# One core, attention and a token mixer in one kernel: the same 2,292 operations in another written-out order

## The chip, the cores and the metric

The kernel runs on one core of one Trainium2 chip. The metric is the device time of one execution in microseconds (us). Lower is better. A profile of one execution is at hand for the kernel before, with the time of each instruction on each engine: TensorE (PE, with its weight loads as PEld), VectorE (DVE), ScalarE (ACT), GpSimd (POOL), and SyncE (SP), whose queue issues all the DMAs here.

## The reference

Four batches, eight heads, 768 tokens, 64 channels a head. Attention with a local window and block summaries comes first, then a mixer over its result `x`:

```
k_sum = max of k over blocks of 32;  v_sum = mean of v over blocks of 32
scores = scale * [q @ k.T within 16 tokens,  q @ k_sum.T + log(32)]
x = softmax(scores) @ [v, v_sum]          # (4, 768, 512) after joining the heads
theta = x @ w_theta
zr, zi = x * cos(theta), x * sin(theta)
u = x + w_tok_r @ zr + w_tok_i @ zi       # over tokens
out = u + max(u @ w_ch, 0)
```

All inputs and outputs are 32-bit floats; the weights reach the core as pairs of 32-bit words of a 64-bit float.

## The kernel before

The work is cut into 24 attention tiles of 128 tokens (six in each of four batches). The kernel records every step as an operation of a `Program`: a function that emits the instructions, the engines that may run it with a cost each, and what it reads and writes. Nothing is scheduled when the kernel is built: `schedule` reads a table, `ORDER`, of 2,292 numbers. A number names an operation, and a letter behind it an engine (`g` GpSimd, `d` VectorE); without a letter the cheapest engine by the recorded costs takes it. The instructions are emitted in this order, so the table sets what stands in front of what on every engine and in the DMA queue, and how buffers of a ring are handed on. Each engine runs its own instructions strictly in that order.

One tile goes through these steps, by the names and lines of the kernel before:

- `S` (line 522): TensorE makes the scores in two PSUM tiles. VectorE adds the mask and takes the row maximum (line 558), ScalarE the exponential (line 562).
- `PT` (line 571): TensorE turns the exponentials; ScalarE or VectorE copies both halves to `e` (line 577).
- `AV` (line 545): TensorE multiplies by the values; `XN` divides by the sum (lines 585 to 595).
- `X` (line 604): TensorE turns the result; copies at lines 308 to 310.
- `TH` (lines 635 and 640): theta; then `PH`, cosine and sine in `zu` (lines 651 to 664); then `Z` (line 670), two instructions a tile that multiply the attention's result by cosine and sine.
- `M` (line 698): mixing over tokens for the first two batches, six steps a half. For the last two batches seven products `MP` (line 813) take fewer multiplications, with operands `hl` split from `zu` (lines 308 to 317). The products add up in a few PSUM banks; VectorE adds a bank to `x` after each product (line 822), and a later product goes on in the same bank.
- `CP` (line 918): the channel product and the output.

At the start the core loads keys (`zu<-kT`, four transfers), queries (`q<-qg`), values for the block means (`x<-vn`, three transfers) and the theta weights (`wth`), then the token weights (`wt<-wtr`, `wt<-wti`), which VectorE turns from 64-bit to 32-bit floats in four steps (lines 400 to 411). The keys' block maxima are a reduction on VectorE (line 445). Five operations `WARM` (line 378, two records each) are multiplications of a tile of zeros that nobody reads. `PRE` (line 449, three operations of four records) makes the block means of the values.

Of the kernel before, what the change touches and what calls it, by code (L numbers as in the profile page):

```python
# [21 lines left out]
NH = H // 2  # L22
# [7 lines left out]
NK = NB + NL  # L30
# [28 lines left out]
224 213 246 225 97 226 104 98 237 215 105 99d 214 109 247 244 216 251 123 217d 111 220d 124g 253 249 252 218 345 227 250 106
221 350 118 228 119g 248 255 125 229 219d 257 254 222d 258 120 297 256 259 260 348g 230 270 121 423g 231 306 261 262 309 122  # L60
263 425g 271 126 351g 135 298 349g 264d 346 313 272 273 274 292 267d 291 300 301 422g 275 265 310 302 127 130 308 115 304 307
299 268 266 305 113 131g 311 269d 303 312 276 314 132 141 529 136g 133 277 315 317 316 352 325 142g 134 326 318 361 232 364
363 137 327 278 112 143 279 424g 116 138 322d 419 328 152 353 144 329 347 365 153g 319 233 139 146 145 354 367 323 330 163 362
355 282 331 368 114 280 283 358 421 147g 284 285 281 339 154 366 155 320 321 337 324d 359 117 164g 128 356 156 360 357 168 369
370 340 332 372 148 380 165 149 371 166 169 381 373 426 420 167 157 170 474 382 374 383 333 150 171 158 334 172 377 159 384
375 400 338 174 129 234 477 376 175g 335 385 378 392 386 160 427 401 393 176 379 387 402 388 177 161 454 455 178 179 703 341
435 403 151 394 389 404 456 180g 181 457 182 458 183 408 459 288g 460 709 390 405 461 462 395 466 409 463 429 467 437 410 411
436 286 430 468 464 412 414 438 431 441 413 415 704 440 469 439 406 442 343g 521 434 428 416 433 407 522 417 418 432 534g 479g
287g 443 480 444 481 741 465 445 446d 535 482 733 475 447 483 485 490 492 493 532 451 489 484 491 486 448 452 523 342g 449
450d 495 496 488 478g 487 497 453d 494 536 537 538 509 510 498 705 586 336 476g 539 499 472g 500d 530 742 501 391 583 564 511  # L70
502 545 540 541 512 707g 706g 548 513 531g 549 506d 503 546 504 547 514 697 542 565 505d 708g 524 551 544 507 550 140 543 533g
584 515 508d 710g 289g 516 552 553 747 711 554 517 556d 587 714 555 712 713 557 734 621 832 715 623 561d 558d 596 588 518 559
716 653g 598 737 519 602 590 592 717 591 597 589 594 833g 748 624 396d 398 599 834g 600 745 615d 718 595 344g 568 562 585 719
397 560 473g 566 603 593 668 601 567 569 665 563d 720 604 746 605 606d 470g 607 735 572 576 570 625 574 626 608 627 738 471g
784 634 617 636 785 616g 618 162 619 629 399g 620 659 736 633 622 786 787d 612d 788 654 835 527g 609 640 836 638 655 789 628
755 721 632 637 610 520 613 656 837g 790 630 631 739 641 525 740 635 611 661 791 838g 526g 614 639 792 657 642 643 793 173
645d 528g 578d 669 644 646 839 678 698g 647d 666 812 658 752 670 841 648 663 667 794d 722 672 813 815d 660g 743 814 795 680
840 676 842 682 945g 580 662 843g 753 816 671 184 684 681 699 817 675 664 673 844g 818 650d 679 651 700 796 744 677 724 819
683 579g 685 723 820 701 727 754 649 674 652d 702 850 845g 581d 729 686 821 582 846g 687 798g 851 756 688 689d 690 757 847 852
853 946 975 765 760 768 848 940 725g 731 859 694 728g 978 854 769 732 822 761 695 976d 691 730 692 860g 977 979 767 797 799  # L80
849 802 766 772 803 943 758 1020 693d 980 770 762 749 759 750 763 1021 696 764 981 800 726 861g 982 1018 575 801 771 751 983
773 984 806 774 855g 856g 947 571 1015 775d 804 810 776 808 823 948 777 1106g 995 996d 858 985 778 828 956 857 941 824 949 998
959 986 957 829 862g 997 953 951 863g 830 999 955 958 952 1000 825 1074 962 864d 573 942g 779 781 831 866 577 988 987 1001 950
782 1019g 960 1002 868 865 780 954 961 991 963 783d 964 867 965 826 944d 966d 1003 809 967 1022 805 968 1004 1077 1031 1005d
877 1034 1050 869 807 870g 992 1006 1053d 993 1023 1051d 871g 969 994 972 1032 872 1052 1016 1075 1035 827 1054 1025 1029 1007
973 878g 970 1024 1033 1055 811 989 1026 971d 1011 1038 873 974d 1028 1056 1027 990 1057 1120g 879g 1030 874g 875 880g 1017
1013 1036 1039 1037 1040 1129 1078 1041d 1058 876 1042 1043 886 1079 1059 1076 1082 1087 887g 1088 1208 1047 1048 881 1080
1128 1081 1209d 1014 1092 1012 1089 882g 1068 1211 1090 1044d 1210 1009 1060d 1061 1045 1170 1212 1127 1008 1093 1083 1063
1066 1213 1086 1010g 888 883 1107 1126 1067 1214 889 1091 1084 1046 1094 1069 1215 1062 1070 890 1049d 1216 1072 1085 1095
1096 884 891g 1130 1097d 885 1217 1139 1064g 1065g 893 1098 1099 1279 1100d 1103d 895 892g 1282 1071 1142 1131 1280 1171 894  # L90
# [164 lines left out]
def c_pool(n, two=True):  # L255
    return (0.18 + n * 2.1e-3) if two else (0.11 + n * 0.9e-3)
# [862 lines left out]
```

## Time and profile before

| | |
|---|---|
| time, median of 3 runs | 438.94 us (438.0 to 439.17) |
| the profiled execution's own time | 436.4 us |
| span of its instructions | 434.7 us |
| TensorE busy | 423.7 us, 97% of the span |
| VectorE busy | 357.9 us, 82% |
| ScalarE busy | 282.0 us, 65% |
| GpSimd busy | 187.8 us, 43% |
| moved by DMA | 100.06 MB, mean 230 GB/s |

The span runs from the first to the last instruction in the trace; 1.7 us of the profiled execution lie around it, and that execution is 2.5 us under the median of the runs. TensorE's end times are modelled, so that an instruction can be shown as busy while the next one already starts.

### The profile page before, as it was taken

Reading aid. Unit: us, or ns where it says so; the run is one execution under the profiler, and the core shown is the slowest. Engines: PE = TensorE matmul, PEld = TensorE weight load, DVE = VectorE, ACT = ScalarE, POOL = GpSimd, SP = SyncE. Lnnn points to the kernel's source line nnn. Section 1 sums busy time; section 2 is a strip of 40 time slices with the busy share of each in tenths; the row PEclk is TensorE's granted clock in tenths of the full one; section 3 lists DMA queues with packets and bytes.
Section 4 is the critical chain, followed back from the end, with each engine's and each line's share of the span. In section 5 each row is a group of like instructions: output and inputs, shape, how many; then the busy total and the mean of one; then the engine's idle time right before and its main releaser. Section 6 shows DMA issues by size and latency. Waiting matters only on the chain.

```text
span 434.7 us, 10048 instructions
## 1 busy us (share of the span) xinstructions
PE 423.7 (97%) x3682; PEld 350.2 (81%) x3682; DVE 357.9 (82%) x958; ACT 282.0 (65%) x616; POOL 187.8 (43%) x193
## 2 busy tenths in 40 slices
PE   6999999999999999999999999999999999999996
PEld 1465565566888888888888898999899899999996
DVE  4899999878687597867667987576888999999996
ACT  1899988686685697868396683588944355554330
POOL 2536311678873425257242555451362220253361
PEclk9999999999999999999999999999999999999999
DMA  7999977978975877786779978772368598300357
GB/s 309 385 352 315 340 258 255 255 231 253 301 256 146 247 226 225 225 239 197 205 245 287 285 226 244 246 235 93 112 221 334 166 335 273 99 18 2 109 199 255
DMA packets 76320, 100.06 MB, mean 230 GB/s; under 512 B 23024, under 2 KB 58864, under 8 KB 76272
## 3 DMA queue, kind: packets, MB, share of 16 engines
q1 hardware_dynamic: 76272, 99.43, 71.3%
q8 instruction: 29, 0.48, 0.5%
q14 instruction: 19, 0.16, 0.1%
HBM read 75.82 MB, written 23.59 MB: 229 GB/s over the span
## 4 chain that ended last, share of the span: by engine, by line
PE 80%; DMA 9%; DVE 7%; ACT 2%; issue 1%; SPq 1%; POOL 0%; POOLq 0%; DVEq 0%; ACTq 0%
PE m L813 20%; PE m L698 17%; PE t L640 11%; PE c L918 7%; PE m L918 6%; PE pa L545 5%; PE s L522 4%; DMA v<-vg 2%; PE pa L571 2%; PE t L604 2%; DMA wt<-wtr 2%; DMA q<-qg 1%; PE t L635 1%; DVE f L408 1%; DMA k<-kg 1%; DMA f<-kT 1%
## 5 line engine op out<-in xcount | busy, mean ns | idle before, releaser
L813 PE MATMUL m<-wt,hl 128*128 128x384 f32 x504 | 96.0, 339 | 1.5 <-ACT hl L308 0.8
L813 PEld LDWEIGHTS m<-wt,hl 128*128 128x128 f32 x504 | 88.0, 188 | 5.2 <-ACT hl L308 1.1
L698 PE MATMUL m<-wt,hl 128*128 128x512 f32 (+1 forms) x432 | 84.3, 340 | 0.0
L698 PEld LDWEIGHTS m<-wt,hl 128*128 128x128 f32 x432 | 68.6, 188 | 10.7
L562 ACT ACTIVATE e<-e,st 128x118 f32<-128x118 f32 x192 | 63.5, 388 | 13.6 <-DVE st L558 12.9
L317 POOL TENSOR_TENSOR hl<-zu,hl 128x512 fp32r<-128x512 f32 x24 | 32.5, 1354 | 45.9 <-DVE st L588 15.4
L558 DVE CUSTOM_DVE_ANT_0 e<-s,cs 128x118 f32<-128x118 f32 x192 | 45.6, 272 | 5.1 <-PE s L522 3.2
L640 PE MATMUL t<-wth,xh 128*128 128x512 f32 x144 | 45.8, 399 | 0.0
L670 DVE TENSOR_TENSOR zu<-xn,zu 128x512 f32<-128x512 f32 x48 | 36.9, 780 | 2.4 <-ACT zu L664 2.2
L698 PE MATMUL m<-wt,zu 128*128 128x512 f32 (+1 forms) x96 | 32.8, 488 | 0.0
L726 POOL TENSOR_TENSOR f<-f 128x192 f32<-128x192 f32 x25 | 16.2, 650 | 35.9 <-DMA f<-f_scratch 8.2
L308 ACT CAST hl<-zu 128x512 fp32r<-128x512 f32 x30 | 18.5, 618 | 20.0 <-PE m L813 13.0
L545 PEld LDWEIGHTS pa<-v,e 118*64 118x64 f32 x768 | 24.7, 137 | 6.9 <-issue 2.5
L698 PEld LDWEIGHTS m<-wt,zu 128*128 128x128 f32 x96 | 17.9, 190 | 14.8 <-issue 13.4
L545 PE MATMUL pa<-v,e 118*64 118x65 f32 x768 | 28.1, 224 | 0.9 <-ACT e L577 0.7
L653 DVE SCALAR_TENSOR_TENSOR zu<-zu,t 128x512 f32<-128x512 f32 x24 | 16.4, 682 | 15.3 <-ACT zu L651 15.3
L726 POOL TENSOR_TENSOR zu<-zu 128x512 f32<-128x512 f32 x16 | 21.5, 1348 | 16.5 <-DVE zu L726 9.5
L640 PE MATMUL t<-wth,xl 128*128 128x512 f32 x72 | 28.4, 395 | 0.0
L317 DVE TENSOR_TENSOR hl<-zu,hl 128x512 fp32r<-128x512 f32 x36 | 27.5, 765 | 0.3 <-ACT hl L308 0.2
L651 ACT ACTIVATE zu<-t,bmagic 128x512 f32<-128x512 f32 x24 | 16.5, 687 | 17.3 <-PE t L640 15.5
L522 PE MATMUL s<-k,q 64*64 64x118 f32 x768 | 25.6, 268 | 2.2 <-DMA q<-qg 1.6
L577 ACT COPY e<-pa 118x512 f32<-118x512 f32 x29 | 16.4, 585 | 16.8 <-PE pa L571 16.5
(181 smaller groups left out, 897.2 us busy)
## 6 DMA issues: line engine op xcount, KB each, us to landing
wt<-s_scratch SPq DMA_DIRECT2D x48, 384.0 KB, 4.7
v<-vg SPq DMA_DIRECT2D x48, 195.0 KB, 4.9
s_scratch<-f SPq DMA_DIRECT2D x24, 384.0 KB, 3.5
k<-kg SPq DMA_DIRECT2D x18, 376.0 KB, 5.2
q<-qg SPq DMA_DIRECT2D x24, 256.0 KB, 5.1
wt<-wti SPq DMA_DIRECT2D x6, 768.0 KB, 10.8
wt<-wtr SPq DMA_DIRECT2D x6, 768.0 KB, 10.2
f<-kT SPq DMA_DIRECT2D x12, 384.0 KB, 4.0
```

What stands on the lines that cost most here:

```text
L308: nc.scalar.copy(dst(), src())
L317: lambda e: V[e].tensor_tensor(dst(), src(), hi().bitcast(F32), op=ALU.subtract), reads, writes, due, port=BOTH)
L522: mm(0.79 * len(pairs) / NP, [lambda p=p, g=g, h=h: nc.tensor.matmul(sc[h].get()[ROW[g], p], q.get()[ROW[h], p, ROW[g]], k.get()[ROW[h], p ...
L545: mm(2 * 0.433 + scores[0] + (0.2 if scores[0] else 0.0), [lambda n=n, g=g, a=a: nc.tensor.matmul(xa[a].get()[ROW[g], n], turned[g].get()[ ...
L558: op({"DVE": 0.205}, lambda eng, n=n: nc.vector.tensor_tensor_reduce(e()[:, n], sc[n % 2].get()[:, 2 * a + n // 2], mask(m), -SCALE, 3.0e3 ...
L562: op({"ACT": 0.288}, lambda eng, n=n: nc.scalar.activation(e()[:, n], e()[:, n], AF.Exp, bias=st.get()[:, n:n + 1], scale=-1.0), [(st, n)] ...
L640: calls = [lambda t=t, xx=xx, k=k, c=c: nc.tensor.matmul(th.get(), xx.get()[:, c], w_th[c].get()[:, k], start=(c == 0 and t == 0), stop=(c ...
L670: op({"DVE": c_dve(DM, "two")}, lambda e, z=z, hc=hc: nc.vector.tensor_tensor(z(), xn[b, i].get().rearrange("p h d -> p (h d)")[:, None, h ...
L698: nc.tensor.matmul(acc[th](), zz, w[:, TT[th]], start=(s == 0 and r == 0 and t == 0 and (th == 0 or c == 0)), stop=(s == NT - 1 and r == 1 ...
L726: lambda e: V[e].tensor_tensor(dst(), x(), y(), op=ALU.add if sign > 0 else ALU.subtract), reads, writes, due, port=BOTH)
L813: calls = [lambda ref=ref, tt=tt, z=z, s=s, j=j, t=t, x=x, k=k, bank=bank, first=first: nc.tensor.matmul(bank[j].get()[:, :HT], z.get()[:, ...
L918: calls = [lambda k=k, t=t, x=x, y=y: nc.tensor.matmul(to.get(), weights[n][x][0]()[:, k, j * P:(j + 1) * P], operands[n].get()[:, y, k], ...
```

## The change

`ORDER` is a new table over the same 2,292 operations; 287 of them stand on another engine than before. The `Z` products may now run on GpSimd as well, and the new table sends 21 of the 48 there. The costs in `SWITCH` and of `PT` are changed too; they are not read when the table is followed.

```diff
 ORDER = """
-8 31 23 0g 17 18 25 27 29 1 24 2 9 39 86 10 26 3 44 28 30 4 32 33 46 45g 47g 50 5 19 35 49 6 48g 7g 87d 51 79 11g 60 12 185 61
...
+17 23 25 0g 1 27 39 8g 24 2 18 3 19 26 44 28 46g 29 45 30 47 9 48 49g 31 4 50 5 15 6 7 20 33 86 13 35 79 51 60 190g 10 14 185
...
-            mm(NH * 0.0545, [lambda n=n, g=g, a=a, e=e: nc.tensor.transpose(tp[g].get()[:NK, NH * a + n], e()[ROW[g], n], ident()[ROW[g], ROW[g]])
+            mm(NH * 0.0575 + 0.03, [lambda n=n, g=g, a=a, e=e: nc.tensor.transpose(tp[g].get()[:NK, NH * a + n], e()[ROW[g], n], ident()[ROW[g], ROW[g]])
...
-            op({"DVE": c_dve(DM, "two")}, lambda e, z=z, hc=hc: nc.vector.tensor_tensor(
+            op({"DVE": c_dve(DM, "two"), "POOL": c_pool(DM)}, lambda e, z=z, hc=hc: V[e].tensor_tensor(
                 z(), xn[b, i].get().rearrange("p h d -> p (h d)")[:, None, hc].broadcast_to((P, 2, HC)), z(), op=ALU.mult),
```

What the table does is best seen in the order of the instructions. In the new kernel every line number from `ORDER` on is one higher (604 is 605).

First place: the DMA queue at the start. Before:

```order
L302 DMA x<-vn 128x2x512
L302 DMA zu<-kT 128x798 x4
L302 DMA q<-qg 128x512
L302 DMA wth_100<-wth 128x1024
L302 DMA x<-vn 128x2x512 x2
L302 DMA wth_150<-wth 128x1024
L302 DMA q<-qg 128x512
```

Now:

```order
L303 DMA zu<-kT 128x798 x3
L303 DMA q<-qg 128x512
L303 DMA zu<-kT 128x798
L303 DMA x<-vn 128x2x512 x2
L303 DMA wth_136<-wth 128x1024
L303 DMA x<-vn 128x2x512
L303 DMA wth_141<-wth 128x1024
L303 DMA q<-qg 128x512
```

The first queries stand behind three transfers instead of five, and the values for the block means behind them; the second `q` still has the same ten transfers in front of it.

TensorE at the same place (`t<-zu` is `WARM`, `pa<-x` is `PRE`, `s` is `S`; a "..." stands for the rest of a half of the first tile's scores). Before:

```order
L378 MATMUL t<-zu 128x512
L449 MATMUL pa_114<-x,vt 24x512 x2
L522 MATMUL s_121<-k,q 64x118
...
L378 MATMUL t<-zu 128x512
L449 MATMUL pa_114<-x,vt 24x512 x4
L522 MATMUL s_201<-k,q 64x118
```

Now:

```order
L379 MATMUL t<-zu 128x512 x2
L523 MATMUL s_117<-k,q 64x118
...
L379 MATMUL t<-zu 128x512
...
L523 MATMUL s_119<-k,q 64x118
L450 MATMUL pa_164<-x,vt 24x512 x6
L523 MATMUL s_212<-k,q 64x118
```

Two `WARM` stand ahead of the first scores, one between their halves, and all of `PRE` behind them; before, a third of `PRE` stood ahead.

Second place: TensorE from the first tile's theta (`t<-xh,x`) to the third tile's `AV` (`pa<-v,e`); `pa<-cs,e` is `PT`, `t<-cs,xn` is `X`. Before:

```order
L635 MATMUL t<-xh,x 128x512
L635 MATMUL t<-xl,x 128x512
L545 MATMUL pa_405<-v,e 64x65 x8
L545 MATMUL pa_414<-v,e 64x65 x8
L635 MATMUL t<-xh,x 128x512
L635 MATMUL t<-xl,x 128x512
L522 MATMUL s_460<-k,q 64x118
...
L571 MATMUL pa_479<-cs,e 118x64
...
L604 MATMUL t<-cs,xn 128x128 x4
L545 MATMUL pa_517<-v,e 64x65 x8
```

Now:

```order
L636 MATMUL t<-xh,x 128x512
L546 MATMUL pa_398<-v,e 64x65 x8
L546 MATMUL pa_407<-v,e 64x65 x8
L636 MATMUL t<-xl,x 128x512
L636 MATMUL t<-xh,x 128x512
L636 MATMUL t<-xl,x 128x512
L572 MATMUL pa_456<-cs,e 118x64
...
L523 MATMUL s_479<-k,q 64x118
...
L605 MATMUL t<-cs,xn 128x128 x4
L546 MATMUL pa_522<-v,e 64x65 x8
```

The fourth tile's scores (`s_479`, before `s_460`) went from ahead of the third tile's `PT` to behind it, and the second tile's `AV` (`pa_398`, before `pa_405`) one theta multiplication forward.

Third place: TensorE in the products of the last batch, where the second, third and fourth of its products meet (`m_4587` and `m_4495`, now `m_4552` and `m_4496`, are the two banks in which all of them add up; three rows are one step of a product). Before:

```order
L813 MATMUL m_4587<-wt,hl 128x384 x9
L813 MATMUL m_4495<-wt,hl 128x384 x3
L813 MATMUL m_4587<-wt,hl 128x384 x9
L813 MATMUL m_4495<-wt,hl 128x384 x9
L813 MATMUL m_4587<-wt,hl 128x384 x6
```

Now:

```order
L814 MATMUL m_4552<-wt,hl 128x384 x6
L814 MATMUL m_4496<-wt,hl 128x384 x9
L814 MATMUL m_4552<-wt,hl 128x384 x9
L814 MATMUL m_4496<-wt,hl 128x384 x9
L814 MATMUL m_4552<-wt,hl 128x384 x9
```

Before, the third row holds the last step of one product and the first two of the next in one bank; now the second row does, in the other bank. In both, TensorE goes from one product to the next in the same bank with nothing in between.

## Rows read from the trace of the kernel before

**Rows 1.** The page, part 1: busy us (share of the span) of each engine.

```profile
PE 423.7 (97%) x3682; PEld 350.2 (81%) x3682; DVE 357.9 (82%) x958; ACT 282.0 (65%) x616; POOL 187.8 (43%) x193
```

**Rows 2.** The page, part 4: the chain that ended last, by engine.

```profile
PE 80%; DMA 9%; DVE 7%; ACT 2%; issue 1%; SPq 1%; POOL 0%; POOLq 0%; DVEq 0%; ACTq 0%
```

**Rows 3.** Timeline of TensorE from the start: start, us, instruction, [idle before].

```profile
1.57 2.08 PE L378 MATMUL t<-zu 128*128 128x512 f32 x2 [1.57 <-DVE zu L376]
4.57 3.58 PE L449 MATMUL pa<-x,vt 128*24 128x512 f32 x4 [0.92 <-DMA x<-vn]
9.73 0.64 PE L522 MATMUL s<-k,q 64*64 64x118 f32 x16 [1.58 <-DMA q<-qg]
...
11.35 0.64 PE L522 MATMUL s<-k,q 64*64 64x118 f32 x16
...
12.97 3.62 PE L449 MATMUL pa<-x,vt 128*24 128x512 f32 x8
16.52 1.04 PE L522 MATMUL s<-k,q 64*64 64x118 f32 x32
```

**Rows 4.** Timeline of TensorE around `X` and `AV` of three tiles.

```profile
30.63 0.66 PE L604 MATMUL t<-cs,xn 128*128 128x128 f32 x4
...
33.02 1.13 PE L635 MATMUL t<-xh,x 128*128 128x512 f32 x2
...
38.46 0.65 PE L604 MATMUL t<-cs,xn 128*128 128x128 f32 x4
...
40.61 1.12 PE L635 MATMUL t<-xh,x 128*128 128x512 f32 x2
...
54.09 0.60 PE L604 MATMUL t<-cs,xn 128*128 128x128 f32 x4
...
55.71 1.04 PE L522 MATMUL s<-k,q 64*64 64x118 f32 x32
```

**Rows 5.** The chain and TensorE's timeline ahead of the seventh tile's scores.

```profile
74.22 5.19 DMA k<-kg
...
80.20 1.04 PE L522 MATMUL s<-k,q 64*64 64x118 f32 x32 [0.59 <-POOL k L499]
```

**Rows 6.** Products of the last batch: two rows of TensorE, one of VectorE.

```profile
345.59 6.76 PE L813 MATMUL m<-wt,hl 128*128 128x384 f32 x36 [0.83 <-ACT hl L308]
352.91 10.71 PE L813 MATMUL m<-wt,hl 128*128 128x384 f32 x60 [0.56 <-DVE x L822]
...
344.94 0.55 DVE L822 TENSOR_TENSOR x<-m,x 128x384 f32<-128x384 f32 x1
```

**Rows 7.** Windows: busy us of PE, PEld, DVE, ACT, POOL; clock, DMA share, GB/s.

```profile
8.00:10.00 2.00, 0.42 (x12) 0.30 (x14) 1.88 (x3) 0.79 (x3) 0.03 (x1) 1.00 1.02 404
...
40.00:60.00 20.00, 20.00 (x152) 11.77 (x149) 19.97 (x42) 19.03 (x36) 4.76 (x4) 1.00 0.93 311
60.00:80.00 20.00, 19.62 (x77) 10.83 (x75) 19.19 (x42) 15.46 (x34) 4.95 (x6) 1.00 0.87 278
```

**Rows 8.** First loads: chain, VectorE's reductions, ScalarE's first exponential.

```profile
3.23 6.37 DMA q<-qg
...
6.93 2.98 DVE L445 TENSOR_REDUCE ks<-zu 128x24 f32<-128x768 f32 x3 [0.51 <-DMA zu<-kT]
...
12.46 0.39 ACT L562 ACTIVATE e<-e,st 128x118 f32<-128x118 f32 x1 [3.10 <-DVE st L558]
```

**Rows 9.** Groups of `Z` and of GpSimd's like product (last number: mean ns); two VectorE rows.

```profile
L670 DVE TENSOR_TENSOR zu<-xn,zu 128x512 f32<-128x512 f32 x48 | 36.9, 780 | 2.4 <-ACT zu L664 2.2
L317 POOL TENSOR_TENSOR hl<-zu,hl 128x512 fp32r<-128x512 f32 x24 | 32.5, 1354 | 45.9 <-DVE st L588 15.4 <-DVE wt L317 14.9 <-DVE hl L310 9.0
...
338.52 0.42 DVE L406 TENSOR_SCALAR zu<-zu 128x512 int32<-128x512 int32 x1
346.72 1.32 DVE L406 TENSOR_SCALAR zu<-zu 128x512 int32<-128x512 int32 x1
```

**Rows 10.** Timeline of TensorE, one `AV` in the first batches.

```profile
105.73 1.22 PE L545 MATMUL pa<-v,e 118*64 118x65 f32 x32 [0.20 <-DVE e L577]
```

More of the change, by code (lines that the diff above doesn't have):

```diff
@@ L59 @@
[L59 to L66, printed above, removed]
@@ new lines @@
+766 979 757 768 731 980 579 695 798g 760 692 767 1020g 946 693 749 770 851g 750 726 940 758 771 772 852g 761 759 847 763 730
+981 732 982 848 696d 769 941 751g 753 764 580d 1015 762 800 581d 773 774 754 853 983 854g 824 799g 984 849 947 577 775d 776
+777 1021 855g 582 956 957 943 995 948 960 802 1016 961 856 998d 949 801 825g 803 996d 859 1106 997 985 806 778 860g 858 959
+999 958 810 804 857 781d 868 951 861g 953 573 1000 962 950 782 944d 1001 862 828 952 1002 779 829 963 808 955 780 954 1003
@@ new lines @@
+1210 1045 1082 1014 990g 1212 1048 1068 1213 1091 1069 1061 1062 886 1075 1066 1088 1214 1092 1083 1129 1094 1170 887 1010
+1126 888g 1067 1086 1084 1089 1085 1046d 1072 1215 1063 1049d 1070 1064g 882 889 1093 1095 883 890g 1216 1096 1217 1128 884
+1098d 1097d 891g 1076 1073 1279 1065g 1218 1099 1202 1130 1219 1110 1282d 1280d 885 893 1103 1100d 892g 1281 1101 895 1139
+1283 1131 894 1143 1141 1071 1284 896 1142 1120g 1145 1135 1108 1228 1132 1140 1285 1102d 1133 1173 897 898 1137 1134 1109 899
@@ new lines @@
+1604g 1353d 1405 1380 1595g 1429 1672 1395 1431 1392 921 1650 1394 1591g 1404 1384d 1660 1403 1119 932 1649 1397 1396 927d
+1402 1651 1298 1592 933g 1435 1444 1433 1386g 1597 1406 1407 1304 1652 1654 1463 1115 1653 1611 1447 1409 1408 1596g 928 1410
+1527 1656 1659 1436 1598 1430g 1662 1655 1411 1528 1439 1664 1414d 1529 1666 1601 1412 934g 1300 1530d 1531 1437 1668 1432
+1446 1413d 1438 935g 1532 929 936g 1381 1415 1607g 1450 1657 1441 1670 1661 1440 930 1533 937g 1663 1608g 1675 1445 1416 1605
@@ new lines @@
+1486d 1582 1488 1508 1691 1766 1627g 1694 1704 1541 1697 1540 1693 1767d 1696 1510 1489 1509 1511 1500 1502 1514 1769 1492d
+1583d 1512 1699 1700 1503 1632 1768 1702 1703 1506 1504 1622 1493 1501 1770 1544 1706 1771 1625 1490 1705 1626g 1623g 1497
+1584 1491 1507 1729 1772 1708 1710 1505 1513 1515 1773 1624g 1709 1494d 1712 1714 1516 1774 1517 1775 1545 1518 1519d 1542
+1520 1554 1555 1776 1780 1628g 1711 1716 1783 1713 1559 1735 1726 1585 1781d 1715 1635g 1718 1546 1521 1522 1548 1586 1640g
+1717 1720 1782 1719 1633 1524 1547 1630 1631 1721 1552 1784 1641 1551 1722 1834g 1785 1525 1732 1556 1738 1724 1723 1786 1557
@@ L140 @@
+2290 2291
 """
@@ L179 @@
     WINDOW, WARM, COOL = 3.41, 0.88, 0.45
-    SWITCH = {("split", "whole"): 0.09, ("split", "block"): 0.16, ("block", "split"): 0.3, ("whole", "block"): 0.09,
-              ("block", "whole"): 0.22, ("whole", "split"): 0.055, ("split", "theta"): -0.008, ("theta", "split"): -0.01,
+    SWITCH = {("split", "whole"): 0.005, ("split", "block"): 0.16, ("block", "split"): 0.3, ("whole", "block"): 0.09,
+              ("block", "whole"): 0.22, ("whole", "split"): -0.024, ("split", "theta"): -0.008, ("theta", "split"): -0.01,
               ("theta", "whole"): -0.006, ("theta", "block"): 0.12, ("block", "theta"): 0.31, ("whole", "theta"): 0.0,
               ("block", "score"): 0.2, ("score", "block"): 0.177, ("score", "split"): 0.185, ("score", "whole"): 0.185, ("score", "theta"): 0.185,
-              ("split", "row"): 0.086, ("whole", "row"): 0.09, ("theta", "row"): 0.177, ("block", "row"): 0.2, ("score", "row"): 0.15,
-              ("row", "split"): 0.185, ("row", "whole"): 0.185, ("row", "theta"): 0.185, ("row", "block"): 0.177, ("row", "score"): 0.15,
+              ("split", "row"): 0.095, ("whole", "row"): 0.15, ("theta", "row"): 0.12, ("block", "row"): 0.2, ("score", "row"): 0.18,
+              ("row", "split"): 0.107, ("row", "whole"): 0.157, ("row", "theta"): 0.13, ("row", "block"): 0.177, ("row", "score"): 0.11,
               ("split", "score"): 0.086, ("whole", "score"): 0.09, ("theta", "score"): 0.177}
```

140 lines of the change are left out of this document (64 added, 76 removed), and 3 rows, old and new, of the table ORDER.

## The prediction, made before the result was known

> **What bounds the kernel now.** I read the busy times first [rows 1]: TensorE works for 423.7 of 434.7 us, and no other engine passes 82%. Then the chain that ended last, by engine [rows 2]: 80% of it is TensorE, 9% DMA and 7% VectorE. The change leaves TensorE's instructions as they are, so only the 11.0 us in which TensorE is idle can be won. The reader is to look for the waits in TensorE's timeline and to ask of each what came last. Four places matter.
>
> At the start the first tile's scores begin at 9.73, when the first queries have landed; a `PRE` operation of four records ran ahead of them, from 4.57, in 3.58 us, and eight records of the same kind took 3.62 us at 12.97 [rows 3]. The granted clock is 1.00 from 8 us on [rows 7]; the first records at half the later rate say that before it TensorE's clock was at the lower of its two levels, 1.2 GHz in place of 2.4. Next come the first tiles' `AV`: from the start of `X` to the theta behind `AV` took 2.39 and 2.15 us for the second and third tile, against 1.62 us from `X` to the next group where nothing waited [rows 4], so 0.77 and 0.53 us are waits. The seventh tile's scores waited 0.59 us for a copy of keys on GpSimd [rows 5]. In the last batch two products waited 0.83 and 0.56 us [rows 6]; the second for VectorE, the first put down to ScalarE, although an addition `x<-m,x` on VectorE ended at 345.49, 0.1 us ahead of it. In both places the product goes on in a bank that VectorE has just read.
>
> Between 40 and 60 us TensorE is full, VectorE has 19.97 and ScalarE 19.03 us of work, GpSimd 4.76; between 60 and 80 us 19.19, 15.46 and 4.95 [rows 7]. So VectorE is the engine that can be late, and GpSimd has room.
>
> **The change part by part.**
>
> *The start.* The first `q` lands at 3.23 + 6.37 = 9.60 us [rows 8]. It is moved past one `x` (512 KB by its shape, 128x2x512 words of four bytes) and one `kT` (399 KB); at the 404 GB/s at which the transfers ran [rows 7] these 911 KB take 2.3 us, so it lands at about 7.3. The fourth `kT` loses 512 KB ahead of it and gains a `q` of 256 KB: 0.6 us earlier. VectorE's four reductions ended at 6.93 + 2.98 = 9.91 [rows 8]; the last one now ends at about 9.3. With two copies of keys on ScalarE of some 0.3 us each the second half of the scores begins at 9.85 (before, 11.35) and ends at 10.4. All of `PRE` stands behind it: twelve records at 3.62/8 = 0.45 us are 5.4 us, to 15.8. Up to the end of the third `x` nine transfers bring 3,900 KB in 9.9 us; before, the 2,364 KB up to the first `q` took 6.0 us at that rate, so the stream began at about 3.6. The third `x` then lands at 13.5, and the records that need it start at 14.0: hidden by 0.5 us. The second `q` has the same transfers ahead and lands at 15.4 by the same count (4,668 KB). So the second tile's scores begin at 15.8 in place of 16.52: **0.7 us earlier**. Bounds: 0, if the third `x` or the copies are a little late, and 1.1, if only the second `q` limits. The first exponential, at 12.46 after a wait of 3.10 us [rows 8], moves with the second half of the scores, by 1.5 us; that time ScalarE can use.
>
> *AV of the first tiles.* The fourth tile's scores now stand between the third tile's `PT` and the second tile's `X`. They take 1.04 us less an overlap of 0.07, as the scores at 16.52 do [rows 3], and lie in front of the place at which TensorE waited 0.77 us: 0.6 regained, since ScalarE's copies there come in another order too. The second tile's `AV` goes forward by one theta multiplication (1.13/2 = 0.56 us a record, two records or so of cover gone) behind two copies on ScalarE; I charge 0.2. The third tile's `AV` is left at its 0.53. **0.4 us won**; bounds −0.8, if the moved `AV` waits for all that it lost in cover, and 1.3, if both waits go.
>
> *Ahead of the seventh tile.* Four `Z` leave VectorE's row ahead of the keys, 4 times 0.78 = 3.1 us [rows 9]. GpSimd has them instead, and was busy for a quarter of its time here [rows 7]: it isn't late. The keys landed at 74.22 + 5.19 = 79.41 and the scores began at 80.20 [rows 5]; the transfer is issued when VectorE frees the buffer, so with 3.1 us less ahead it is issued earlier: **0.6 us won**, all of the wait. Bounds: 0, if the queue and not the buffer holds it, and 0.6.
>
> *`Z` on GpSimd.* A `Z` takes 780 ns on VectorE; GpSimd's product of the same shape 1354 ns [rows 9]. 21 times each: VectorE loses 16.4 us of work, GpSimd gets 28.4 and would be busy 187.8 + 28.4 = 216 us, half the span. VectorE's 16.4 us lie beside TensorE and are worth nothing by themselves. What hangs on them is the path theta, `PH`, `Z`, `M`: 0.57 us longer wherever the moved `Z` is the last of its tile. Between a tile's theta and the `M` that reads its `Z` TensorE has another tile's `PT`, `AV` or scores to do, some microseconds; I charge half of one place: **−0.3**. Bounds: 0 if all are hidden, and −2.3 for four places without cover.
>
> GpSimd's products also hold VectorE up: a conversion step took 0.42 us alone and 1.32 us while a GpSimd product ran [rows 9]. The Trainium skill, GPSIMD Engine Reference, § 8 Key points, says that GpSimd shares its SBUF interfaces with VectorE, and that they contend with VectorE instructions in a two-port mode or with two SBUF inputs; the trace agrees, with 0.90 us for that pair. By that rule 21 products at 0.90 us each would cost VectorE 18.9 us, and the move would give it nothing. By the rows I count on some of them only: 0.90 us each for a third, 6.3 us, so VectorE still gains some 10 us, off the path.
>
> *The other waits.* A wait of 0.20 us at an `AV` stands behind a copy on VectorE [rows 10], which now has less work ahead of it: **0.2**, bounds 0 and 0.2. In the last batch TensorE still goes from one product to the next in the same bank with nothing in between, at both places. VectorE's addition of 0.55 us [rows 6] must be done first in either order: **0**, bounds 1.4 (both waits gone) and −0.6 (one addition held by 0.55 us more).
>
> The sum is 0.7 + 0.4 + 0.6 − 0.3 + 0.2 = 1.6 us. The profiled execution's span would go from 434.7 to 433.1 and its time from 436.4 to 434.8. It lies 2.5 us under the median of the runs; taken from that, 438.94 − 1.6 = **437.3 us**. Differences under 0.3%, 1.3 us, can't be told from no change here.
>
> **The rivals.** *A, the forecast:* 437.3, own range 436.0 to 438.6: each term may be off by half the way to its bound, and not all to the same side.
>
> *B, the waits are only moved.* ScalarE and VectorE are full from 40 to 60 us [rows 7]; what the start wins is waited for at the next exponential or `AV`, and the moved `AV` and `Z` wait for as much as the others regain. For it: 19.03 and 19.97 of 20 us on two engines. Against it: ScalarE has room again from 60 us on. Then only the 0.2 of the middle and half of the seventh tile's 0.6 are left, less the 0.3 of `Z`: 0.2, so 438.7.
>
> *C, the waits vanish with those of the products.* Start at its bound of 1.1, `AV` 1.3, the seventh tile 0.6, the middle 0.2, products 1.4, nothing lost by `Z`: 4.6 us, 434.3. For it: VectorE has less work before the additions. Against it: the bank.
>
> *D, slower: the clock at the start.* In the order before, `PRE` kept TensorE busy from 4.57 to 8.15, and the next records ran at the full rate. Now two `WARM` stand first; at the 2.08 us that one took from 1.57 [rows 3] they end at about 5.7, and TensorE stands nearly empty to 9.85, but for half of the scores and one `WARM`. If the clock is at the lower level then, twelve `PRE` records take 0.90 in place of 0.45 us and the scores' second half 0.6 more: 6.0 us in all, 443.3; at half of that 3.0 us, 440.3. It decides from about 2.9 us on, where the 1.6 of the forecast are gone and 0.3% lost besides, that is with five of the twelve records and the scores at the lower rate. Against it: the two `WARM` in a row are 4.1 us of unbroken work at the same place at which before 2.08 us and a gap of 0.92 stood [rows 3], so the clock may rise as early. The Trainium skill, TensorE: Matmul & The Clock Gate, Part 1: The HAM clock gate, has it that the low level is the default, that activity lifts it and idling brings it back. By that rule the gap of some 4 us in the new order speaks for D; the trace, with its lower rate to 8 us and its full rate from 9.73 on, agrees with the first half of the rule and shows no fall.
>
> **How the numbers follow.** A 0.46, B 0.23, C 0.16, D 0.15. The bound for faster is 437.6. Of A 0.28 lie below it and 0.18 within 0.3%; of B 0.01, 0.20, and 0.02 slower; C is faster; of D 0.14 are slower, 0.01 same. Together faster 0.45, same 0.39, slower 0.16. The range goes from 434.3, which leaves out half of C, to 440.3, which leaves out half of D: 0.16 outside.
>
> **What would show it.** The first scores begin between 7.3 and 8.5, their second half near 9.85, `PRE` takes 5.4 us in one piece and the second tile's scores begin near 15.8; D shows as `PRE` records of 0.9 us there. From `X` to theta behind the second tile's `AV` about 1.6 us plus the scores; about 0.2 us of wait at the first tile's or moved `AV`. No wait for GpSimd's keys ahead of the seventh tile. `Z` on GpSimd at about 1.35 us, and a wait of about 0.3 us at the first `M`. Two waits of some 0.8 and 0.6 us where the last batch's products meet. The forecast is wrong if a new wait of more than 1 us stands in the first 60 us or at the batches' ends, or if the products' waits are gone.

## The result: 1.5% slower, and the profile after

The changed kernel takes 444.89 us (median of 6 runs, 442.42 to 445.66), the kernel before 437.96 beside it: ratio 1.0147, 95% interval 1.0118 to 1.0177. The forecast was 437.3, its range 434.3 to 440.3. The profiled execution took 443.41 us with a span of 441.7, 7.0 more than before. Medians, here and below, are over all runs; a ratio leaves out runs over 1.5% above the fastest of their kernel, and only c5w10 has such (four of ten; the others' median is 445.49).

Page, part 1, of the changed kernel (answers to [rows 1]):

```profile
PE 426.7 (97%) x3682; PEld 351.4 (80%) x3682; DVE 358.6 (81%) x950; ACT 284.2 (64%) x604; POOL 200.7 (45%) x202
```

The work is the same and VectorE is as busy as before. Where do 7 us arise? TensorE is busy for 3.0 us more and idle for 4.0 us more (15.0 for 11.0). At the following points it has the same instructions behind it in both kernels. The scores of the second tile begin 1.80 us later than before (18.32 against 16.52 [rows 3]), of the fifth 2.02 (39.44, 37.42), of the seventh 2.87 (83.07 against 80.20 [rows 5]), of the tenth 3.93 (108.42, 104.49); the second product of the last batch 6.85 (352.44 against 345.59 [rows 6]), TensorE's last instruction 6.92. So about 2 us are lost at once, and the rest piecemeal, nothing of it given back.

TensorE's timeline at the start of the changed kernel (answers to [rows 3]):

```profile
1.53 3.78 PE L379 MATMUL t<-zu 128*128 128x512 f32 x4 [1.53 <-DVE zu L377]
7.88 1.07 PE L523 MATMUL s<-k,q 64*64 64x118 f32 x16 [2.56 <-DMA q<-qg]
8.87 2.08 PE L379 MATMUL t<-zu 128*128 128x512 f32 x2
10.88 1.06 PE L523 MATMUL s<-k,q 64*64 64x118 f32 x16
11.87 6.52 PE L450 MATMUL pa<-x,vt 128*24 128x512 f32 x12
18.32 1.04 PE L523 MATMUL s<-k,q 64*64 64x118 f32 x32
```

The first scores come 1.8 us earlier, within the forecast's 7.3 to 8.5. But half of the scores takes 1.07 us where it took 0.64, two `WARM` records 2.08 where they take 1.12 at 20.29, and the twelve `PRE` records 6.52 in place of 5.4: TensorE is at 1.2 GHz. Its records go from 0.85 to 0.43 us apart at about 14.3 us. Windows of the same stretch (columns as in [rows 7]):

```profile
12.00:14.20 2.20, 2.20 (x3) 0.35 (x3) 1.70 (x17) 1.86 (x6) 0.29 (x1) 1.00 1.05 402
14.40:18.00 3.60, 3.60 (x10) 0.79 (x8) 3.27 (x7) 1.89 (x6) 0.99 (x3) 1.00 1.05 337
```

Three records in 2.2 us, then ten in 3.6, and the clock column says 1.00 in both: ahead of the first entry of a trace it has nothing to show. There the durations tell the clock, not the column. Behind it, from 20 to 437 us, the column says 1.00, so what this run loses there is not the clock's.

The waits of TensorE behind the start, picked from its timeline:

```profile
33.53 0.66 PE L605 MATMUL t<-cs,xn 128*128 128x128 f32 x4 [0.52 <-DVE zu L654]
...
41.81 0.40 PE L546 MATMUL pa<-v,e 118*64 118x65 f32 x4 [0.37 <-ACT f L401]
...
77.68 1.56 PE L699 MATMUL m<-wt,zu 128*128 128x512 f32 x4 [0.29 <-POOL zu L671]
...
83.07 1.04 PE L523 MATMUL s<-k,q 64*64 64x118 f32 x32 [0.21 <-DMA k<-kg]
...
87.70 1.04 PE L523 MATMUL s<-k,q 64*64 64x118 f32 x32 [1.01 <-DMA k<-kg]
...
124.95 1.15 PE L546 MATMUL pa<-v,e 118*64 118x65 f32 x30 [0.34 <-DVE e L578]
...
218.45 1.15 PE L546 MATMUL pa<-v,e 118*64 118x65 f32 x30 [0.31 <-DVE e L578]
...
264.32 0.97 PE L814 MATMUL m<-wt,hl 128*128 128x384 f32 x4 [0.21 <-DVE x L823]
...
301.24 1.15 PE L546 MATMUL pa<-v,e 118*64 118x65 f32 x30 [0.36 <-DVE e L578]
...
352.44 6.48 PE L814 MATMUL m<-wt,hl 128*128 128x384 f32 x36 [1.19 <-issue]
359.68 1.49 PE L814 MATMUL m<-wt,hl 128*128 128x384 f32 x7 [0.76 <-DVE x L823]
```

None is large. Behind the start of the second tile's scores all waits add up to 6.7 us, before to 2.9; of the 5.1 us lost there the other 1.3 stand in no wait that the timeline shows. Three `AV` wait for a copy of the turned exponentials on VectorE. Its timeline at the second of them:

```profile
215.92 0.95 DVE L466 TENSOR_REDUCE vt<-f 128x24 f32<-128x768 f32 x1 [0.74 <-DMA f<-vT]
216.85 0.95 DVE L446 TENSOR_REDUCE ks<-f 128x24 f32<-128x768 f32 x1
217.72 0.68 DVE L578 COPY e<-pa 118x512 f32<-118x512 f32 x1
218.31 0.68 DVE L654 SCALAR_TENSOR_TENSOR zu<-zu,t 128x512 f32<-128x512 f32 x1
```

VectorE stands idle until a load for the next batch lands, makes two reductions, and only then the copy, for which `PT` had ended at about 216.9, 0.8 us earlier. The waits of VectorE (total us, times, longest) say the same for all tiles; the kernel before, then the changed one:

```profile
DVE e L577 <- PE pa L571: 10.9, 10, 2.7
```

```profile
DVE e L578 <- PE pa L572: 5.3, 9, 1.4
```

Idle time in front of these copies is VectorE's lead where TensorE waits for it next; it has halved.

### The profile page after: what moved, and what is told of

Same layout as the page of the kernel before. It is cut to its first block, busy times and chain, and to the rows that moved or that the text cites. A ratio compares the mean times of both kernels' runs of the same rounds, so it can differ in the third digit from the quotient of the medians.

```text
span 441.7 us, 10042 instructions
## 1 busy us (share of the span) xinstructions
PE 426.7 (97%) x3682; PEld 351.4 (80%) x3682; DVE 358.6 (81%) x950; ACT 284.2 (64%) x604; POOL 200.7 (45%) x202
## 4 chain that ended last, share of the span: by engine, by line
PE 61%; DVE 14%; DMA 9%; ACT 7%; issue 4%; POOL 3%; SPq 1%; DVEq 0%; POOLq 0%; ACTq 0%
PE m L699 15%; PE m L814 12%; PE t L641 9%; PE c L919 5%; PE m L919 5%; PE pa L546 4%; DMA f<-vT 3%; PE s L523 3%; DMA f<-kT 2%; PE t L605 2%; PE pa L572 2%; ACT e L563 2%; PE pa L450 1%; PE t L636 1%; DVE hl L318 1%
## 5 line engine op out<-in xcount | busy, mean ns | idle before, releaser
L699 PE MATMUL m<-wt,hl 128*128 128x512 f32 (+1 forms) x432 | 85.9, 341 | 0.0
L318 POOL TENSOR_TENSOR hl<-zu,hl 128x512 fp32r<-128x512 f32 x24 | 31.3, 1313 | 34.2 <-DVE wt L318 16.6
L671 POOL TENSOR_TENSOR zu<-xn,zu 128x512 f32<-128x512 f32 x21 | 27.6, 1320 | 31.4 <-DVE wt L412 7.2
L309 ACT CAST hl<-zu 128x512 fp32r<-128x512 f32 x38 | 23.0, 616 | 24.3 <-PE m L814 15.8
L654 DVE SCALAR_TENSOR_TENSOR zu<-zu,t 128x512 f32<-128x512 f32 x24 | 16.4, 683 | 19.2 <-ACT zu L652 19.2
L546 PE MATMUL pa<-v,e 118*64 118x65 f32 x768 | 29.0, 224 | 1.4 <-DVE e L578 1.0
L727 POOL TENSOR_TENSOR f<-f 128x192 f32<-128x192 f32 x23 | 14.9, 648 | 32.6 <-DVE f L727 8.8
L523 PEld LDWEIGHTS s<-k,q 64*64 64x64 f32 x768 | 20.4, 136 | 10.9 <-issue 6.8
L641 PEld LDWEIGHTS t<-wth,xh 128*128 128x128 f32 x144 | 23.9, 188 | 3.1 <-issue 0.3
```

The source lines that it names most:

```text
L309: nc.scalar.copy(dst(), src())
L318: lambda e: V[e].tensor_tensor(dst(), src(), hi().bitcast(F32), op=ALU.subtract), reads, writes, due, port=BOTH)
L523: mm(0.79 * len(pairs) / NP, [lambda p=p, g=g, h=h: nc.tensor.matmul(sc[h].get()[ROW[g], p], q.get()[ROW[h], p, ROW[g]], k.get()[ROW[h], p ...
L546: mm(2 * 0.433 + scores[0] + (0.2 if scores[0] else 0.0), [lambda n=n, g=g, a=a: nc.tensor.matmul(xa[a].get()[ROW[g], n], turned[g].get()[ ...
L641: calls = [lambda t=t, xx=xx, k=k, c=c: nc.tensor.matmul(th.get(), xx.get()[:, c], w_th[c].get()[:, k], start=(c == 0 and t == 0), stop=(c ...
L671: op({"DVE": c_dve(DM, "two"), "POOL": c_pool(DM)}, lambda e, z=z, hc=hc: V[e].tensor_tensor(z(), xn[b, i].get().rearrange("p h d -> p (h ...
```

## The experiments

Two theories at the outset: the **clock** (the start, about 2 us) and **queues** (what stands ahead on VectorE and in the DMA queue, the rest). Rivals: a later stage takes up what the start loses; the products on GpSimd cost it all.

| run | us (median) | before beside it | ratio, 95% |
|---|---|---|---|
| h1, old start | 442.65 | 438.75 | 1.0102 (1.005 to 1.0154) |
| h2, new start | 439.24 | 438.75 | 1.0021 (0.9996 to 1.0046) |
| w6, longer warming | 444.80 | 438.75 | 1.0139 (1.0081 to 1.0197) |
| zd, `Z` on VectorE | 447.59 | 438.75 | 1.0204 (1.015 to 1.0258) |
| w10, no gap | 448.03 | 438.46 | 1.0214 (1.0168 to 1.026) |
| h2w10 | 439.40 | 438.46 | 1.0035 (1.0008 to 1.0063) |
| c5, five moves | 443.50 | 438.46 | 1.0109 (1.0073 to 1.0145) |
| c5w10 | 446.07 | 438.46 | 1.0123 (1.0083 to 1.0163) |
| ld, loads forward | 445.53 | 438.56 | 1.0162 (1.013 to 1.0193) |
| bank | 441.52 | 438.56 | 1.0059 (1.0034 to 1.0085) |
| s1, new first part | 446.76 | 437.97 | 1.0223 (1.0183 to 1.0263) |
| s3, old first part | 447.07 | 437.97 | 1.0222 (1.0198 to 1.0246) |
| bw, old order, warming | 437.84 | 437.97 | 1.0000 (0.9981 to 1.0018) |
| changed kernel again | 443.81 | 437.97 | 1.0150 (1.011 to 1.019) |
| eo2, old engines | 474.26 | 438.94 | 1.0802 (1.0763 to 1.0842) |
| oe2, new engines | 496.59 | 438.94 | 1.1303 (1.1262 to 1.1345) |

**The start exchanged (h1, h2).**

```diff
 h1
-all 2,292 operations in the new order
+the first 100 in the old order, the rest in the new one
 h2: the first 100 in the new order, the rest in the old one
```

> The first 100 operations in the order and on the engines of before, the other 2,192 in the new order. Clock theory (2.2 of the 7 us are lost in the first 20 us, because TensorE's clock rises at 14.3 us and not at 8.7, and the loss is carried to the end): the second tile's scores begin near 16.5 and the time is 442.0 to 443.0, some 2 us under the changed kernel. Rival (a later stage has slack that takes up what the start loses, and the loss lies in the later waits alone): the time stays within 0.8 us of the changed kernel's.

> The first 100 operations in the new order, the other 2,192 as before. Clock theory: the clock rises at about 14 us, the second tile's scores begin near 18.3, and the time is about 2 us over the kernel before, 440. Rival (slack later takes it up): within 0.8 us of before.

With the old start the second tile's scores are back at 16.51, and the time falls by 2.2 us in the median. But the runs overlap (441.91 to 445.11, the changed kernel's 442.42 to 445.66), and in the profile most of it goes back: 3.32 us behind before at the tenth tile's scores, where the changed kernel is 3.93, and 5.9 at TensorE's last instruction. The new start in the old order costs only 0.5 us in the median, not clear of none, though its scores came at 17.36 in the profile. So the start carries a third of the loss at most, and it costs less in front of the old order. Windows of h2:

```profile
6.00:9.00 3.00, 0.72 (x17) 0.60 (x18) 1.04 (x2) 0.52 (x2) 0.00 (x0) 1.00 0.99 347
9.20:12.50 3.30, 3.25 (x19) 0.85 (x18) 1.70 (x13) 0.85 (x4) 2.69 (x9) 0.50 1.04 411
12.60:16.00 3.40, 3.40 (x10) 0.79 (x9) 2.35 (x13) 3.29 (x11) 0.88 (x3) 1.00 1.05 408
```

Here the clock had risen by 6 us; TensorE worked 0.72 of 3 us, then half the clock was granted.

**More warming (w6, w10, h2w10, bw).**

```diff
-        for _ in range(K["WARM"]):
-            mm(..., [one product], ...)
+        for n in range(K["WARM"]):
+            mm(..., [one product] * (1, 4, 2, 1, 1)[n], ...)      # w10, h2w10; w6: 2 if n == 1
```

bw doubles the first in the old order, and moves the second ahead of the first scores.

> The changed kernel, its second warming operation with four records in place of two, so that TensorE works until about 7 us instead of 5.3 while it waits for the queries anyway. Clock theory: the clock rises by about 8 us, the block means take 5.2 us in place of 6.5, the second tile's scores begin between 16.2 and 16.7 and the time falls by 1.5 to 2 us, to about 443. Rival (the loads set the start, the third load of values and the second queries): the second tile's scores stay near 18 and the time stays within 0.5 us.

> The changed kernel, its second warming operation with eight records and its third with four (two each in the changed kernel), so that TensorE works through from 1.5 us to the second half of the first scores at about 10.5. Clock theory, after the last four runs (the clock rises between 5 and 6 us when TensorE has worked on end, and falls again because it then waits): the clock rises by 6 us and stays at 1.00, the twelve records of block means take 5.2 us, the second tile's scores begin between 16.0 and 16.6, and the time is 1.5 to 2.2 us under the changed kernel's, 442.7 to 443.4. Rival (the clock falls for another reason than the gap): 0.50 is granted in some stretch before 16 us as before, and the time stays within 0.7 us of 444.9.

> The first 100 operations in the new order with the longer warming of the run before, the other 2,192 as in the kernel before. Clock theory: with the clock kept at 1.00 the new start is worth what the prediction's first term said, 0 to 0.7 us under the kernel before, and about 1 us under the same hybrid with the short warming; the second tile's scores begin between 15.8 and 16.6. Rival (the new start is slower for its loads or its ScalarE work): 0.5 us or more over the kernel before.

> The kernel before; its first warming operation with four records in place of two, its second moved ahead of the first scores, so that TensorE has work from 1.5 us on with one gap less. Clock theory: the clock rises by 7 us and stays, the second tile's scores begin at 16.5 or earlier in each profile, and the time is 0 to 1 us under before with less spread. Rival (the warming only delays the block means and the scores): 0.5 us or more over before.

Without a gap the clock went as the theory says (in w6, which kept a gap of 1.94 us, it rose and fell again); the time did not. The profiles, by when the second tile's scores began:

| start | scores at, us | TensorE's clock |
|---|---|---|
| new | 18.32, 18.18, 18.16 (changed twice, ld) | low until about 14 |
| new | 18.96, 17.36, 17.43 (zd, h2, s1), 17.10 (w6) | up at 5 to 6, 0.50 again from 8 to 9 on |
| new | 15.77 (c5) | up at 5.7, stays |
| old | 16.52, 16.51, 16.23 (before, h1, s3) | up at 7.8 to 8.7, stays |
| old | 19.14 (bank) | low until 15.8 |
| without a gap | 16.32, 16.76, 16.90 (w10, h2w10, c5w10) | up at 5 to 6.5, stays |
| old, one gap less | 16.09 (bw) | up at 5.4, stays |

All three starts without a gap kept the clock, and so did bw, with gaps of 1.16 and 0.83 us; seven of eight with the new gap did not, nor one of four with the old. The old start is not safe either: in the four runs with other engines (below) the clock came late or fell each time, with the scores at 18.21 and 17.44 with the new start and at 17.88 and 18.03 with the old. Yet w10 is 3 us slower than the changed kernel and h2w10 no better than h2; at 0.9 us over before its rival holds. In w10's profile the gain goes back at the fourth tile:

```profile
42.12 1.80 PE L546 MATMUL pa<-v,e 118*64 118x65 f32 x32 [1.55 <-DMA v<-vg]
```

```profile
39.00:42.50 3.50, 1.53 (x35) 1.10 (x29) 3.44 (x10) 3.27 (x6) 0.83 (x1) 1.00 1.02 321
42.60:46.00 3.40, 3.40 (x29) 2.25 (x25) 3.40 (x5) 3.35 (x7) 0.00 (x0) 0.50 1.03 364
46.00:50.00 4.00, 4.00 (x11) 1.95 (x11) 3.84 (x15) 3.36 (x8) 1.93 (x3) 1.00 0.98 324
```

`AV` waits 1.55 us for its values, while the DMA engines are full (1.02); TensorE works 1.53 of 3.5 us, and then half the clock is granted. The values land at 41.98, in the changed kernel at 41.67: a start that is earlier for TensorE alone meets loads that are not. In w6 the same `AV` waits 1.61 us, and half the clock follows. w10 has a second such place, at the seventeenth tile:

```profile
222.02 1.15 PE L546 MATMUL pa<-v,e 118*64 118x65 f32 x30 [1.90 <-DVE e L578]
```

```profile
223.50:226.90 3.40, 3.40 (x14) 2.92 (x13) 2.99 (x15) 2.25 (x4) 1.35 (x2) 0.50 1.03 316
```

bw, an edit to the kernel before, costs nothing and gains nothing.

**`Z` back on VectorE (zd).**

```diff
-190g ... (21 numbers of Z with the letter g)
+190 ...
```

> The changed kernel's order, but all 48 products of attention's result with cosine and sine on VectorE. If GpSimd's longer products and its hold on VectorE cause the later waits: at least 1.5 us faster, 443.4 or less, and the wait for a product on GpSimd ahead of a mixing step at 77.7 is gone. Rival (VectorE, which would get 16 us more work, is the engine that is late): 1 to 4 us slower, with longer waits of TensorE behind VectorE's copies and divisions.

2.7 us slower than the changed kernel, with all four runs above the changed kernel's six in the result: the rival holds. VectorE is busy for 370.3 us, 11.7 more. In this order GpSimd is not what costs; VectorE without that help is later still.

**Single moves (c5, c5w10, ld).** Rows of c5 on two engines, as examples:

```diff
 VectorE, seventeenth tile
+L578 COPY e<-pa
 L446 TENSOR_REDUCE ks<-f
-L578 COPY e<-pa
 SyncE, eighth tile
+L303 DMA k<-kg
 L303 DMA f<-vT
-L303 DMA k<-kg
```

> The changed kernel with five operations moved in front of those that they queue behind, all else as it is: the copy of the turned exponentials on VectorE at the tenth, seventeenth and twenty-third tile, one load of keys on SyncE's queue (eighth tile), and the fifth tile's divisions ahead of a reduction that waits for its load. Queue theory (these waits come from what stands ahead on VectorE and in SyncE's queue, and each adds to the end): the waits of 0.34, 0.31, 0.36, 1.01 and 0.22 us ahead of AV, scores and X are gone and the time falls by 2.0 to 3.5 us, to about 442. Rival (the engines' work is the limit, and a wait taken away comes back at the next place): less than 0.8 us.

> The changed kernel with the five moved operations and the longer warming. If the two causes add: 3.5 to 5.5 us under the changed kernel, 439.4 to 441.4, near the kernel before. If they share one slack: no more than the better of the two alone, 442 or above.

> The changed kernel with the five moves of the earlier run and, besides, the loads of the fourth tile's values ahead of a load of weights, the seventh tile's keys ahead of a load for the maxima, and two reductions on VectorE behind the copy at the seventeenth tile. Load theory (the new order puts loads late in the queue; the fourth tile's AV began 0.13 us after its values had landed in four profiles, the seventeenth tile's copy stood behind reductions whose loads had just landed): the waits at these places are under 0.3 us, the time is 2.5 to 5 us under the changed kernel's, 440 to 442.4, and the spread of the runs is smaller than 4 us. Rival (waits come back elsewhere): 443 or more.

c5 is 1.4 us faster than the changed kernel in the median, inside neither theory's bounds and not clear of the spread (441.15 to 445.78), and its profile had the one good clock. There the start is what the prediction described:

```profile
7.36 0.64 PE L523 MATMUL s<-k,q 64*64 64x118 f32 x16 [2.04 <-DMA q<-qg]
...
9.86 0.63 PE L523 MATMUL s<-k,q 64*64 64x118 f32 x16 [0.81 <-ACT k L500]
10.51 5.33 PE L450 MATMUL pa<-x,vt 128*24 128x512 f32 x12
15.77 0.46 PE L523 MATMUL s<-k,q 64*64 64x118 f32 x8
```

Behind it as much is lost as in the changed kernel: 0.75 us ahead of before at the second tile's scores, 4.6 behind at TensorE's last instruction. The five waits are gone, but 1.09 us stand at the fourth `AV` (0.37 in the changed kernel), 0.58 at the seventh tile's scores (0.21) and 0.68 at an `X` (none): the moves show no gain behind the start. c5w10, slower than c5, waited 1.30 us at the seventeenth `AV`, since another reduction still stood ahead of the copy:

```profile
219.86 1.15 PE L546 MATMUL pa<-v,e 118*64 118x65 f32 x30 [1.30 <-DVE e L578]
```

ld moved that too, and won nothing (445.53). Its timeline:

```profile
85.03 1.35 PE L523 MATMUL s<-k,q 64*64 64x118 f32 x32 [2.18 <-POOL k L500]
...
112.43 1.04 PE L523 MATMUL s<-k,q 64*64 64x118 f32 x32 [1.66 <-DMA q<-qg]
...
223.73 0.66 PE L605 MATMUL t<-cs,xn 128*128 128x128 f32 x4 [1.08 <-DVE zu L654]
```

The wait for the fourth tile's values is gone, and so is that of the seventeenth `AV`; but the keys moved ahead made the load for the maxima late, and GpSimd's copy of the maxima with it (2.18 us of wait, where the changed kernel had 0.21); and the reductions put behind the copy now stand ahead of `L654`, for which `X` waits. The rival holds: a wait taken away comes back at the next operation that the same late load or full engine holds.

**Products of the last batch (bank).** One bank's last steps first, then the other's, and the next product begins in the first:

```diff
 L814 ... m0, step 21
-L814 ... m0, step 22
 L814 ... m2, step 23
+L814 ... m0, step 22
 L814 ... m0, step 23
-L814 ... m0, next product
 L814 ... m2, next product
+L814 ... m0, next product
```

> The kernel before; only in the last batch, where its second, third and fourth products meet, one bank's steps are finished first, and the next product begins in that bank while the other's last steps run, with VectorE's additions in the same order as the banks. If the additions alone cause the waits of 0.83 and 0.56 us there: both are under 0.2 us and the time is 1.0 to 1.5 us under before. Rival (the next product's operands, from ScalarE or the loads, are late as well): TensorE still waits there, and the gain is under 0.5 us.

The first wait of [rows 6] is gone, but TensorE now waits for the weights' load and, at the next product, longer for VectorE:

```profile
352.31 0.59 PE L814 MATMUL m<-wt,hl 128*128 128x384 f32 x2 [1.35 <-DMA wt<-s_scratch]
...
360.36 0.94 PE L814 MATMUL m<-wt,hl 128*128 128x384 f32 x4 [1.61 <-DVE x L823]
```

The rival holds, and the kernel is 3 us slower than before, not 1 us faster; the start of this profile had a late clock besides (19.14), and half the clock follows the first of these waits.

**Two parts (s1, s3), and the changed kernel again.**

```diff
 s1
-all in the old order
+the first 670 operations (110 us) in the new order, the rest in the old one
 s3: the first 670 in the old order, the rest in the new one
```

> The first 670 operations (some 110 us) in the new order, the other 1,622 as before. If the later loss arises anew in each stage: the span lies 3.5 to 4.5 us over the kernel before's profile at 110 us and does not grow after it, and the time is about 442. If it all comes from the first stages: as slow as the changed kernel, 444 or more. If the new first part is harmless and the later part costs: under 440.

> The first 670 operations as before, the other 1,622 in the new order. If the later loss arises anew in each stage: nothing lost up to 110 us against before, then some 2.5 to 3 us, time about 441.3. If all comes from the first stages: within 0.8 us of before. If the later part costs most: 443 or more.

> The changed kernel as it is, once more. If the clock's rise and falls differ from run to run: a profile in which the clock rises at 5 to 6 us, falls again at 8 to 10 and the second tile's scores begin at 17 to 19, or stays and they begin near 15.8; the granted clock over the runs between 0.992 and 1.00. If they are a fixed trait of the order: a rise at 14.3 us again and the scores at 18.3.

Each time meets the highest of its forecasts (444 or more, 443 or more), though the two can't both be right: they come from the seam, from operations that one order has done early and the other counts on. TensorE at the seam of s1, then of s3:

```profile
127.25 0.27 PE L572 MATMUL pa<-cs,e 64*118 64x64 f32 x1 [3.77 <-ACT xn L594]
```

```profile
121.60 0.68 PE L572 MATMUL pa<-cs,e 64*118 64x64 f32 x16 [2.32 <-ACT zu L652]
```

The timelines still tell what was asked. s1 is 4.25 us behind before at the eighth tile's scores, 10.66 at the twelfth's, behind the seam, and 10.8 at the end: the old order loses nothing more. s3 is 0.85 behind at the tenth's, and 7.47 at the end, so the new order's second part loses again, the seam's 2.3 and some 4 more. As far as kernels with a seam can tell, the loss arises anew in the stages of the new order. The changed kernel again had a late clock (scores at 18.18), so for this very order that is more than an accident of one run; yet h2 and s1, with the same first 100 operations, had it up at 5 to 6.

**Engines against order (eo2, oe2).** A first pair, 496.77 and 506.52 us, put 71 and 72 operations on ScalarE that belong on VectorE. (A number without a letter goes to the first engine by name, not to the cheapest, as the text on the kernel says.) They tell one thing: beside the pair that follows, 71 and 72 of 2,292 operations on another engine cost 22 and 10 us.

> The new order, but each operation on the engine that it had before (287 of them differ, the 21 products on GpSimd among them). If the choice of engines is what costs the later microseconds: at least 2 us faster than the changed kernel. Rival (the order, of the loads above all, is what costs): within 1.5 us of the changed kernel, or slower, since the order was made for the other engines.

> The old order with the new engines. If the engines are what costs: 2 us or more slower than before, 440.5 or above. Rival (the order costs): within 1.5 us of before.

With all engines right:

```diff
 eo2
-each operation on the engine of the new table
+each operation on the engine of the old table, in the new order
 oe2: the old order, the engines of the new table
```

> The new order, each operation on the engine that it had before, this time all of them. If the choice of engines costs the later microseconds: at least 2 us faster than the changed kernel. Rival (the order costs, and was made for its engines): as slow as the changed kernel or slower, 444 or more; the run with only the 48 products back on VectorE took 2.7 us more.

> The old order with the new engines, all of them. If the engines cost: 2 us or more over before, and less than the changed kernel's own 6.5. Rival (order and engines belong together): slower than both kernels, 446 or more.

474.26 and 496.59 us: either half alone is far worse than both kernels. Order and engines belong together, and what either costs of the 6.9 us these runs can't tell.

## Why the prediction was wrong

The profile's span is 8.6 us over the forecast of 433.1: some 2.5 us at the start, and some 6 behind it, where 0.9 was to be won and 5.1 were lost.

- *The start* is the step that failed first: "twelve records at 3.62/8 = 0.45 us" took a rate at the full clock for a place at which it had yet to rise. The first scores (7.88 for 7.3 to 8.5) were right; with the clock up, in c5, all was (7.36, 9.86, 15.77 for 7.3, 9.85, 15.8). Rival D named the mechanism, at 0.15, and its sign. It cost 2.5 us against the forecast of 15.8, near its lower price of 3.0: 1.1 in `PRE` (6.52 for 5.4), the rest in scores, warming and the queries' landing. That activity lifts the clock and idling brings it back (Trainium skill, TensorE: Matmul & The Clock Gate, Part 1: The HAM clock gate) agrees with the trace in both halves: in h2 TensorE worked 0.72 of 3.00 us, and 0.50 was granted next.
- *AV of the first tiles*, 0.4 won: none. The `AV` behind the second tile's `X` (it is the third tile's, at 34.12) had no wait, as forecast, and the moved one 0.2; but `X` waited 0.52 us ahead of it, and the fourth tile's `AV` 0.37 for its values' load, which landed at 41.67. In w10 the profile names that load; before, too, the third tile's `AV` began at 31.46, 0.14 us behind the landing of its values at 31.32. So the 0.77 us of [rows 4] were, at least in part, a load's, not ScalarE's.
- *Ahead of the seventh tile*, 0.6 won: lost. "The transfer is issued when VectorE frees the buffer, so with less ahead it is issued earlier" failed: the keys were issued at 77.21, 3.0 us later than at 74.22 (TensorE was 2.0 us late already at the fifth tile), and the eighth tile's at 80.99, behind a load in the same queue. 1.2 us of waits stand where there were 0.59. I counted VectorE's work and not the DMA queue.
- *`Z` on GpSimd*, 0.3 lost: 0.29, at 77.68. That VectorE shares its SBUF interfaces with GpSimd (Trainium skill, GPSIMD Engine Reference, § 8 Key points) would have made the move worth nothing, by the price of 0.90 us each; in this order it is worth 2.7 us (zd). The groups, with a mean of 1320 ns for 1354:

```profile
L671 POOL TENSOR_TENSOR zu<-xn,zu 128x512 f32<-128x512 f32 x21 | 27.6, 1320 | 31.4 <-DVE wt L412 7.2 <-DVE st L559 6.4 <-DVE zu L671 5.4
...
L671 DVE TENSOR_TENSOR zu<-xn,zu 128x512 f32<-128x512 f32 x27 | 19.5, 733 | 2.8 <-ACT zu L665 2.6
```

- "VectorE still gains some 10 us": it is busy for 358.6 us in place of 357.9. `Z` took 17.4 us less (36.9 [rows 9] to 19.5), but of the other 266 operations that changed engine, 117 came to VectorE and 104 left it. For the 21 alone the estimate was fair: put back, they make VectorE 11.7 us busier (zd). I had costed 21 of 287. On this the growing lead rested, and with it the *other waits*, 0.2 won: new ones of 0.3 each at three `AV`.
- *The products*, 0: 1.19 and 0.76 for 0.83 and 0.56, inside the bound of −0.6.
- *The range* ended at 440.3, since only D had a price on that side. What lay beyond is a loss that no rival priced: B let waits move at no net loss, D put all on the start, and here there are many waits of 0.2 to 1 us, each carried to the end.

What stays open: why the same start has the clock up at 5 us in one run and at 14 in another; whether the two stretches at half the clock in w10's profile are what makes its other runs slower too; where the 1.3 us outside the waits are; and which of the many moves costs how much, since none was taken back alone at a gain clear of the spread.

## What to carry to other kernels

Where an order is searched as a whole, cost all that moved, or say that it is not costed: the sum of the few moves one understands had the wrong sign. Count, ahead of each operation that the bounding engine waits for, the loads in the queue and what its engine must wait for first; the engine's work alone does not tell when it comes. A rate measured behind the start is no rate for the start: look at what TensorE does in the microseconds ahead.

## What was not expected of the hardware

The granted clock is part of the spread from run to run. Of the ten runs of the changed kernel six had a mean clock of 0.987 to 0.996 over the span, of the 80 runs of the kernel before that stand beside the experiments, eight. In c5 two runs at 1.000 took 441.15 and 442.14 us, two at 0.991 and 0.994 took 445.78 and 445.29. It is not all of the spread: the changed kernel took 442.42 us at 0.994 and 445.66 at 0.999, and bw, as fast as before, has seven of twelve runs at 0.996 or less. A wait of 1.55 us at one `AV` was followed by a stretch at half the clock (w10, at 42.6 us), and so were waits of 1.90 (w10), 1.61 (w6), 1.30 (c5w10), 2.18 (ld), 1.35 (bank) and 3.77 us (s1); behind waits of 1.66 (ld) and 2.32 us (s3) the clock stayed at 1.00. So a wait can cost more than its length.
